# Ring slots at multiples of 256 bytes, and the result in two PSUM banks: a decode block with attention and a gated MLP

## The chip, the cores and the metric

The kernel runs on one core of a Trainium2 chip. The metric is the device time of one execution in microseconds (us); a run's time is compared as the median of several. The engines are named as in the profile: PE (matmul), PEld (its weight loads), DVE, ACT and POOL (vector, scalar and general engines) and SP, whose queue issues nearly all loads.

## The reference, cut to what matters

One token with 576 features is normalized. The sum of three things is the output: the token itself, attention over the last 4096 entries of a cache, and a gated MLP.

```python
xn = layernorm(x)                                   # x: 1 x 576
q = (xn @ wq)                                       # 32 heads of 128
k, v = k_cache[:, :, -4096:], v_cache[:, :, -4096:] # 16 heads, each for two of q
o = softmax(q k^T * 128 ** -0.5) v
A = o.reshape(1, 4096) @ wo                         # wo: 4096 x 576
z = gelu(xn @ w_in)                                 # 4608
g = w_sp * layernorm(z[2304:]) + b_sp
B = (z[:2304] * g) @ w_out                          # w_out: 2304 x 576
out = x + A + B                                     # 1 x 576, bf16
```

All is bf16. One execution must read 51 MB: wq 4.7, K 16.8, w_in 5.3, V 16.8, w_out 2.7 and wo 4.7.

## The kernel before, in words

**Loads.** All large loads are issued by SP, in the order in which they are written in the code (lines 76 to 106): wq in two pieces; K for four heads; w_in in three pieces; then K and V in turn, two heads (2,048 KB) to a load; w_out in one piece; wo in six pieces of 9, 8, 6, 4, 3 and 2 rows for each partition. Each load goes to a slot of a ring (`ring_tile`, L70) of RING = 7 slots, each of 20,736 bytes in every partition. A load waits until the readers of its slot's last contents are done. In the tile pools' order (const, work, ring, ktpool) the ring begins after the constants and the work tiles, and its first slot lies at byte 45,440 of each partition, which is 128 past a multiple of 256. A row of wo is 1,152 bytes, 4.5 times 256; partition p holds rows 32p to 32p + 31, so a piece that begins at an odd row begins 128 past a multiple in DRAM. The four pieces from rows 9, 17, 23 and 27 do.

**Order.** The schedule is written by hand. `for j in range(HKV)` takes the 16 K heads in turn. `t_head` (L245) transposes K on DVE in two halves; `s_head` (L253) computes scores with eight matmuls of 512 columns. Each four heads are a group: `sm_a` finds the maxima (DVE) and the exponentials (ACT), `sm_b` transposes them (DVE) and spreads them with sixteen ACT copies (`PT`, L295), `pv` (L303) multiplies them with V in 32 matmuls, and `yb` (L313 to L324) scales the result and turns it into Y. Between the first heads stand the MLP's matmuls (`z_mms`), its activation (`z_rest`) and its second normalization (`z_norm`), whose small matmul (L361) writes a corner of the accumulator's bank.

**The end.** The accumulator `acc` is one PSUM bank. The output's first 288 columns are summed in its partition 0 and the last 288 in partition 32. `out_mms` (L406) issues for each row of w_out or wo two matmuls of one weight column and 288 columns: one in the column tile at 0, one in the column tile at 32. After the last group's `pv` come two thirds of w_out (`out_hv(0)`, `out_hv(1)`, 24 matmuls), the last `yb`, the last third (12 matmuls) and the 32 rows of wo (64 matmuls). Then DVE (L429) copies the first 144 columns of the 33 partitions 0 to 32 into `res`, ACT (L430) the other 144, and two DMAs of 576 bytes, one issued by SP (L432) and one by ACT (L433), store partitions 0 and 32.

Of the kernel before, what the change touches and what calls it, by code (L numbers as in the profile page):

```python
# [8 lines left out]
FP32 = mybir.dt.float32  # L9
BF16 = mybir.dt.bfloat16  # L10
# [4 lines left out]
D = 576  # L15
# [14 lines left out]
CW = D // 2  # L30
# [3 lines left out]
RING = 7  # L34
# [5 lines left out]
def kernel(  # L40
# [14 lines left out]
    nc = tc.nc  # L55
    P = nc.NUM_PARTITIONS

    const = ctx.enter_context(tc.tile_pool(name="const", bufs=1))
    work = ctx.enter_context(tc.tile_pool(name="work", bufs=2))
    ring = ctx.enter_context(tc.tile_pool(name="ring", bufs=RING))  # L60
    ktpool = ctx.enter_context(tc.tile_pool(name="ktpool", bufs=3))
    ps_s = ctx.enter_context(tc.tile_pool(name="ps_s", bufs=1, space=bass.MemoryType.PSUM))
    ps_o = ctx.enter_context(tc.tile_pool(name="ps_o", bufs=1, space=bass.MemoryType.PSUM))
    ps_m = ctx.enter_context(tc.tile_pool(name="ps_m", bufs=1, space=bass.MemoryType.PSUM))
    ps_a = ctx.enter_context(tc.tile_pool(name="ps_a", bufs=1, space=bass.MemoryType.PSUM))

    ctx.enter_context(tc.manual_schedule())

# [19 lines left out]
    def load_n(src, per, lo, n, name):  # L88
        v = ring_tile(f"{name}{lo}", n, D)
        nc.sync.dma_start(v, src.rearrange("(p t) n -> p t n", t=per)[:, lo:lo + n, :])  # L90
        return [(lo + t, v[:, t, :]) for t in range(n)]
# [10 lines left out]
        V.update(load_kv(A_v_cache, m, "v"))  # L102
    wout_sb = load_n(B_w_out, NF, 0, NF, "wout")
    wo_sb = []
    for n in (9, 8, 6, 4, 3, 2):
        wo_sb += load_n(A_wo, 32, len(wo_sb), n, "wo")


# [2 lines left out]
    xrow = const.tile([1, D], BF16, name="xrow")  # L111
# [14 lines left out]
    ones_b = const.tile([1, P], BF16, name="ones_b")  # L126
# [28 lines left out]
    for n in range(2):  # L155
# [3 lines left out]
    ops = ps_o.tile([P, 512], FP32, name="ops")  # L159
    nc.vector.memset(ops[:], 0.0)  # L160

    mx = const.tile([P, 32], FP32, name="mx")
    nc.gpsimd.memset(mx[:], 0.0)
    lx = const.tile([P, 32], FP32, name="lx")
    nc.gpsimd.memset(lx[:], 1.0)
# [13 lines left out]
        out=junk[:], in0=x_col[:], in1=x_col[:], scale=1.0, scalar=0.0,  # L179
# [23 lines left out]
    for s, wv in wq_sb:  # L203
        for g in range(4):
            nc.tensor.matmul(  # L205
                qps[32 * g:32 * g + 2, :], lhsT=XT[:, s, :], rhs=wv[:, 512 * g:512 * (g + 1)],
                start=(s == 0), stop=(s == NS - 1), tile_position=(0, 32 * g),
# [12 lines left out]
    for k in range(4):  # L220
        for be in range(4):
            nc.tensor.matmul(
                qps2[:, k, be, :].rearrange("p (r g) -> p r g", r=2),
                lhsT=q_rep[0:NR, 2 * k + be // 2, be % 2].rearrange("p a d -> p (a d)"),
                rhs=idq, start=True, stop=True)
# [14 lines left out]
    def t_head(j):  # L240
        kT = ktpool.tile([P, NT, 2, 32, 2], BF16, name=f"kT{j}", tag="kT")
        src = K[j].rearrange("p t d -> p (t d)").bitcast(FP32)
        dst = kT[:].rearrange("p t b k e -> p (t b k e)").bitcast(FP32)
        for hf in range(2):
            nc.vector.transpose(dst[:, 1024 * hf:1024 * (hf + 1)], src[:, 1024 * hf:1024 * (hf + 1)])  # L245
        KT[j] = kT

    def s_head(j):
        g, i = divmod(j, GK)
        kv = KT.pop(j)[:].rearrange("p t b k e -> p b e t k")  # L250
        for hf in range(2):
            for be in range(4):
                nc.tensor.matmul(  # L253
                    S[g % 2][32 * i:32 * i + 8, hf, :],
                    lhsT=Qb[:, j, be].rearrange("p a h -> p (a h)"),
                    rhs=kv[:, be // 2, be % 2, 16 * hf:16 * hf + 16, :],
                    start=(be == 0), stop=(be == 3), tile_position=(0, 32 * i),
                )
# [13 lines left out]
    def sm_a(g):  # L272
        s = S[g % 2]
        nc.vector.tensor_reduce(out=mx[:, 0:1], in_=s[:], op=ALU.max, axis=mybir.AxisListType.XY)  # L274
        bk = spread(mx, mb, g, ALU.max, "m")
        nm = work.tile([P, 1], FP32, name=f"nm{g}", tag="nm")
        nc.vector.tensor_scalar_mul(nm[:], bk[:, 0:1], -SCALE)  # L277
        p = work.tile([P, 1024], BF16, name=f"p{g}", tag="p")
        nc.scalar.activation(p[:], s[:].rearrange("p a n -> p (a n)"), ACT.Exp, bias=nm[:, 0:1], scale=SCALE,  # L279
                             accum_out=lx[:, 0:1])  # L280
        st[g] = {"p": p}

    def sm_b(g):
        d = st[g]
        pt = work.tile([P, NT, 32], BF16, name=f"pt{g}", tag="pt")
        nc.vector.transpose(pt[:].rearrange("p t x -> p (t x)"), d["p"][:])  # L286
        lbk = spread(lx, lb, g, ALU.add, "l")
        rs = work.tile([P, 1], FP32, name=f"rs{g}", tag="rs")
        nc.vector.reciprocal(rs[:], lbk[:, 0:1])
        PT = work.tile([P, GK, NT, 2], BF16, name=f"PT{g}", tag="PT")  # L290
        pt4 = pt[:].rearrange("p t x -> p (t x)").bitcast(FP32).rearrange("p (t x) -> p t x", x=16)
        PT4 = PT[:].rearrange("p i t h -> p (i t h)").bitcast(FP32).rearrange("p (i t) -> p i t", i=GK)
        for i in range(GK):
            for a in range(4):
                nc.scalar.copy(PT4[32 * a:32 * a + 32, i, :], pt4[32 * i:32 * i + 32, :, a])  # L295
        d["PT"] = PT
        d["rs"] = rs
# [29 lines left out]
    def z_mms():  # L327
        zps = ps_a.tile([P, 2, NF], FP32, name="zps", tag="a")
        for s, wv in win_sb:
            wt = wv.rearrange("k (p t) -> k t p", t=NF)  # L330
            for t in range(NF):
                nc.tensor.matmul(zps[:, :, t], lhsT=wt[:, t, :], rhs=XT[:, s, :],  # L332
                                 start=(s == 0 and t == 0), stop=(s == NS - 1 and t == NF - 1),
                                 skip_group_check=True)
        return zps
# [21 lines left out]
        )  # L357
        return G, sz

    def z_norm(G, sz, psz):  # L360
        nc.tensor.matmul(psz[:, 0:2], lhsT=ones_f[:], rhs=sz[:], start=True, stop=True)  # L361
        mz = const.tile([P, 4], FP32, name="mz")
        nc.vector.tensor_scalar_mul(mz[:, 0:2], psz[:, 0:2], 1.0 / FH)
        nc.vector.tensor_mul(mz[:, 2:3], mz[:, 0:1], mz[:, 0:1])
        nc.vector.tensor_sub(mz[:, 2:3], mz[:, 1:2], mz[:, 2:3])
        nc.vector.tensor_scalar_add(mz[:, 2:3], mz[:, 2:3], EPS)
        nc.gpsimd.tensor_tensor(out=mz[:, 3:4], in0=mz[:, 2:3], in1=mhalf[:], op=ALU.pow)
        zn = const.tile([P, NF], FP32, name="zn")
        nc.vector.tensor_scalar(out=zn[:], in0=G[:, 1], scalar1=mz[:, 0:1], scalar2=mz[:, 3:4],
                                op0=ALU.subtract, op1=ALU.mult)  # L370
        nc.vector.tensor_scalar(out=zn[:], in0=zn[:], scalar1=wb[:, 0:1], scalar2=wb[:, 1:2],
                                op0=ALU.mult, op1=ALU.add)
        hv = const.tile([P, NF], BF16, name="hv")
        nc.vector.tensor_mul(hv[:], G[:, 0], zn[:])
        return hv

    for j in range(HKV):
        t_head(j)
        g, o = divmod(j, GK)
        if g > 0 and o == 0:  # L380
            sm_a(g - 1)
        if g > 0 and o == 1:
            sm_b(g - 1)
        s_head(j)
        if j == GK - 1:
            zps = z_mms()
        if j == GK + 1:
            G, sz = z_rest(zps)
            acc = ps_a.tile([P, 512], FP32, name="acc", tag="a")
            out_t = acc[:, 0:CW]  # L390
            nc.vector.memset(out_t, 0.0)
        if j == GK + 2:
            hv = z_norm(G, sz, acc[:, 384:386])
            for n in range(2):
                nc.tensor.matmul(
                    out_t[32 * n:32 * n + 1, :], lhsT=ones_b[:, 0:1], rhs=xrow[:, CW * n:CW * (n + 1)],
                    start=True, stop=False, tile_position=(0, 32 * n),
                )
        if g > 1 and o == 0:
            yb(g - 2)  # L400
        if g > 0 and o == 3:
            pv(g - 1)

    def out_mms(lhs, col, wv, last):
        for n in range(2):
            nc.tensor.matmul(  # L406
                out_t[32 * n:32 * n + 1, :], lhsT=lhs[:, col:col + 1], rhs=wv[:, CW * n:CW * (n + 1)],
                start=False, stop=last, tile_position=(0, 32 * n),
            )

    def out_hv(c):
        for t, wv in wout_sb[6 * c:6 * c + 6]:
            out_mms(hv, t, wv, False)
# [10 lines left out]
    for t, wv in wo_sb:  # L424
        out_mms(Y, t, wv, t == 31)

    res = const.tile([P, CW], BF16, name="res")
    half = CW // 2
    nc.vector.tensor_copy(res[0:33, 0:half], out_t[0:33, 0:half])  # L429
    nc.scalar.copy(res[0:33, half:CW], out_t[0:33, half:CW])  # L430
    out_row = out.flatten_outer_dims()
    nc.sync.dma_start(out_row[:, 0:CW], res[0:1, :])  # L432
    nc.scalar.dma_start(out_row[:, CW:D], res[32:33, :])  # L433

# [1 line left out]
_INS = ['A_x', 'A_k_cache', 'A_v_cache', 'A_wq', 'A_wo', 'B_x', 'B_w_in', 'B_w_sp', 'B_b_sp', 'B_w_out']  # L436
# [26 lines left out]
```

## Time and profile before

| What | Value |
|---|---|
| Time, median of 3 runs | 129.92 us (129.87 to 129.98) |
| Time of the profiled execution | 130.34 us |
| Its span, first to last instruction | 128.6 us |
| Mean granted clock of PE | 0.795 of full |
| PE, DVE, ACT busy | 74.6, 74.2, 23.2 us |
| Loaded | 50.96 MB |
| Mean rate over the span | 396 GB/s |
| Last wo piece (2 rows), issue to landing | 11.8 us |
| Stores issued at | 126.37 us |

The profiled execution's own time is longer than its span by the 1.74 us around the first and the last instruction, and longer than the median by 0.42 us. Times inside the profile count from the first instruction. An engine's busy time says little by itself: what matters is which wait ends last in each stage.

Two kinds of record are used beside the views. Each DMA packet has a queue, a start, a size and a duration. Each matmul has a start; its end is modelled, so the distance between starts says how fast matmuls follow one another.

### The profile page before, as it was taken

The numbers are of one execution on the slowest core, as the hardware profiler recorded it, in microseconds if no ns is written. First come the engines' busy times: TensorE is split into PE (matmuls) and PEld (weight loads), VectorE is DVE, ScalarE is ACT, GpSimd is POOL, SyncE is SP. The second block draws the span as 40 slices with busy tenths as digits, with TensorE's granted clock in tenths as the row PEclk, the third lists the DMA queues.
The fourth block names the chain that finished last, engine by engine and source line by source line (L and its number), as shares of the span: only waits on it lengthen the run. The fifth ranks groups of instructions, "written<-read, shape, count | busy, mean of one in ns | idle before, by whom it ended". The sixth has DMA issues, their size and how long they took to land.

```text
span 128.6 us, 1586 instructions
## 1 busy us (share of the span) xinstructions
PE 74.6 (58%) x610; PEld 33.4 (26%) x610; DVE 74.2 (58%) x156; ACT 23.2 (18%) x77; POOL 3.6 (3%) x19
## 2 busy tenths in 40 slices
PE   0002831399999696008459456991579802876681
PEld 0002301132699521002113111231113301234340
DVE  6604135999000599464399799997998557050000
ACT  1200011000000003920000308303074049100000
POOL 4301000000000000000100000000000000000000
PEclk9999997569995559955867976999555995589677
DMA  5999999999999999999999999999999999999940
GB/s 115 421 434 423 410 426 421 443 426 426 430 403 426 410 418 426 415 423 428 421 421 423 423 423 418 418 426 415 421 426 415 423 444 437 412 417 411 409 159 0
DMA packets 6177, 51.06 MB, mean 397 GB/s; under 512 B 535, under 2 KB 538, under 8 KB 1050
## 3 DMA queue, kind: packets, MB, share of 16 engines
q1 hardware_dynamic: 6082, 50.96, 95.3%
q8 instruction: 5, 0.08, 0.3%
q10 hardware_dynamic: 88, 0.00, 0.0%
q14 instruction: 2, 0.02, 0.0%
HBM read 50.96 MB, written 0.00 MB: 396 GB/s over the span
## 4 chain that ended last, share of the span: by engine, by line
issue 41%; DMA 28%; DVE 15%; PE 8%; ACT 4%; POOLq 0%; POOL 0%; SPq 0%; ACTq 0%; DVEq 0%
DMA k<-in_A_k_cache_dram 12%; DMA wo<-in_A_wo_dram 9%; DMA x<-in_A_x_dram 7%; DVE kT L245 6%; PE S L253 4%; ACT PT L295 3%; PE ops L303 2%; DVE pt L286 2%; DVE mx L274 2%; ACT p L279 1%; DVE on L317 1%; DVE om L313 1%; PE yps L320 1%; PE ps_x L182 0%; POOLq L458 0%
## 5 line engine op out<-in xcount | busy, mean ns | idle before, releaser
L253 PE MATMUL S<-kT,Qb 128*8 128x512 bf16 x128 | 40.8, 491 | 21.5 <-DVE kT L245 20.8
L245 DVE STREAM_TRANSPOSE kT<-k 128x1024 f32<-128x1024 f32 x32 | 37.1, 1212 | 11.1 <-DMA k<-in_A_k_cache_dram 11.0
L253 PEld LDWEIGHTS <-Qb 128*8 128x8 bf16 x128 | 11.7, 98 | 46.6 <-issue 38.2
L295 ACT COPY PT<-pt 32x32 f32<-32x32 f32 x64 | 15.4, 241 | 13.7 <-DVE pt L286 12.9
L279 ACT ACTIVATE p<-S,nm 128x1024 bf16<-128x1024 f32 x4 | 4.5, 1114 | 55.6 <-DVE nm L277 55.6
L303 PE MATMUL ops<-v,PT 128*8 128x512 bf16 x128 | 13.4, 456 | 0.4 <-ACT PT L295 0.4
L332 PEld LDWEIGHTS <-win 128*128 128x128 bf16 x162 | 10.1, 162 | 0.4 <-issue 0.4
L332 PE MATMUL zps<-XT,win 128*128 128x2 bf16 x162 | 10.2, 202 | 0.0
L320 PE MATMUL yps<-on,sel 128*32 128x32 f32 x32 | 2.1, 220 | 10.2 <-DVE on L317 10.2
L406 PE MATMUL acc<-wo,Y 128*1 128x288 bf16 x64 | 6.3, 348 | 2.8 <-DMA wo<-in_A_wo_dram 2.7
L274 DVE TENSOR_REDUCE mx<-S 128x1 f32<-128x1024 f32 x4 | 4.8, 1206 | 1.7 <-PE S L253 1.6
L429 DVE CAST res<-acc 33x144 bf16<-33x144 f32 x1 | 0.3, 299 | 9.5 <-PE acc L406 9.5
L172 PE MATMUL ps_x<-x,rmat 64*128 64x9 bf16 x1 | 0.2, 163 | 9.7 <-DMA x<-in_A_x_dram 9.7
L286 DVE STREAM_TRANSPOSE pt<-p 128x1024 bf16<-128x1024 bf16 x4 | 4.8, 1210 | 1.4 <-ACT p L279 1.4
L303 PEld LDWEIGHTS <-PT 128*8 128x8 bf16 x128 | 4.1, 91 | 5.9 <-issue 2.2
L313 DVE SCALAR_TENSOR_TENSOR om<-ops,rs,dmask 128x512 f32<-128x512 f32 x4 | 3.0, 742 | 4.2 <-PE ops L303 4.2
L406 PEld LDWEIGHTS <-Y 128*1 128x1 bf16 x64 | 3.3, 97 | 5.7 <-issue 3.9
L320 PEld LDWEIGHTS yps<-on,sel 128*32 128x32 f32 x32 | 1.7, 132 | 11.7 <-DVE on L317 9.6
L205 PE MATMUL qps<-wq,XT 128*2 128x512 bf16 x36 | 4.0, 627 | 1.0 <-DVE XT L196 1.0
L317 DVE TENSOR_REDUCE on<-om 128x128 f32<-128x512 f32 x4 | 4.1, 1030 | 0.1
L216 DVE CAST q_rep<-qps 128x512 bf16<-128x512 f32 x2 | 1.4, 692 | 4.6 <-PE qps L205 3.9
L214 ACT CAST q_rep<-qps 128x512 bf16<-128x512 f32 x2 | 1.2, 585 | 14.8 <-DVE q_rep L216 14.8
(90 smaller groups left out, 37.1 us busy)
## 6 DMA issues: line engine op xcount, KB each, us to landing
k<-in_A_k_cache_dram SPq DMA_DIRECT2D x8, 2048.0 KB, 22.3
v<-in_A_v_cache_dram SPq DMA_DIRECT2D x8, 2048.0 KB, 21.5
win<-in_B_w_in_dram SPq DMA_DIRECT2D x3, 1728.0 KB
wout<-in_B_w_out_dram SPq DMA_DIRECT2D x1, 2592.0 KB
wq<-in_A_wq_dram SPq DMA_DIRECT2D x1, 2560.0 KB
wq<-in_A_wq_dram SPq DMA_DIRECT2D x1, 2048.0 KB, 13.3
wo<-in_A_wo_dram SPq DMA_DIRECT2D x1, 1296.0 KB
wo<-in_A_wo_dram SPq DMA_DIRECT2D x1, 1152.0 KB
```

What stands on the lines that cost most here:

```text
L245: nc.vector.transpose(dst[:, 1024 * hf:1024 * (hf + 1)], src[:, 1024 * hf:1024 * (hf + 1)])
L253: nc.tensor.matmul(S[g % 2][32 * i:32 * i + 8, hf, :], lhsT=Qb[:, j, be].rearrange("p a h -> p (a h)"), rhs=kv[:, be // 2, be % 2, 16 * hf ...
L274: nc.vector.tensor_reduce(out=mx[:, 0:1], in_=s[:], op=ALU.max, axis=mybir.AxisListType.XY)
L279: nc.scalar.activation(p[:], s[:].rearrange("p a n -> p (a n)"), ACT.Exp, bias=nm[:, 0:1], scale=SCALE, accum_out=lx[:, 0:1])
L286: nc.vector.transpose(pt[:].rearrange("p t x -> p (t x)"), d["p"][:])
L295: nc.scalar.copy(PT4[32 * a:32 * a + 32, i, :], pt4[32 * i:32 * i + 32, :, a])
L303: nc.tensor.matmul(ops[32 * i:32 * i + 8, :], lhsT=d["PT"][:, i, 4 * tb:4 * tb + 4, :].rearrange("p t h -> p (t h)"), rhs=V[GK * g + i][:, ...
L313: nc.vector.scalar_tensor_tensor(out=om[:].rearrange("p c d -> p (c d)"), in0=ops[:], scalar=d["rs"][:, 0:1], in1=dmask[:].rearrange("p c ...
L317: nc.vector.reduce_sum(on[:], om[:].rearrange("p c d -> p d c"), axis=AXX)
L320: nc.tensor.matmul(yps[32 * g:32 * g + 32, :], lhsT=sel[:, dq, :], rhs=on[:, 32 * dq:32 * dq + 32], start=(dq == 0), stop=(dq == 3), tile_ ...
L332: nc.tensor.matmul(zps[:, :, t], lhsT=wt[:, t, :], rhs=XT[:, s, :], start=(s == 0 and t == 0), stop=(s == NS - 1 and t == NF - 1), skip_gr ...
L406: nc.tensor.matmul(out_t[32 * n:32 * n + 1, :], lhsT=lhs[:, col:col + 1], rhs=wv[:, CW * n:CW * (n + 1)], start=False, stop=last, tile_pos ...
```

## The change

The ring's pool is opened first, behind a pool of one tile (`mx`, 128 bytes), so that the first slot lies at byte 16,640, a multiple of 256; as a slot is 81 times 256 bytes, every slot does. The pieces of wo have 10, 8, 6, 4, 2 and 2 rows, so that each begins at an even row. The accumulator is two tiles of one partition in two PSUM banks; both use the column tile at 0. There is no fill with zeros: the two matmuls with x open the sums, and they stand before the scores of head 6 rather than after them and the norm's matmul. The norm's matmul has a bank of its own. DVE copies the first half and ACT the second, 288 columns each, into one row, which SP stores with one DMA of 1,152 bytes.

```diff
+    lead = ctx.enter_context(tc.tile_pool(name="lead", bufs=1))
+    ring = ctx.enter_context(tc.tile_pool(name="ring", bufs=RING))
     const = ctx.enter_context(tc.tile_pool(name="const", bufs=1))
     work = ctx.enter_context(tc.tile_pool(name="work", bufs=2))
-    ring = ctx.enter_context(tc.tile_pool(name="ring", bufs=RING))
...
+    ps_b = ctx.enter_context(tc.tile_pool(name="ps_b", bufs=1, space=bass.MemoryType.PSUM))
...
-    for n in (9, 8, 6, 4, 3, 2):
+    for n in (10, 8, 6, 4, 2, 2):
         wo_sb += load_n(A_wo, 32, len(wo_sb), n, "wo")
...
-    mx = const.tile([P, 32], FP32, name="mx")
+    mx = lead.tile([P, 32], FP32, name="mx")
...
-    def z_norm(G, sz, psz):
+    def z_norm(G, sz):
+        psz = ps_m.tile([P, 512], FP32, name="psz", tag="m")
...
-            acc = ps_a.tile([P, 512], FP32, name="acc", tag="a")
-            out_t = acc[:, 0:CW]
-            nc.vector.memset(out_t, 0.0)
+            acc = [ps_a.tile([1, 512], FP32, name="acc0", tag="a"), ps_b.tile([1, 512], FP32, name="acc1")]
+            for n in range(2):
+                nc.tensor.matmul(acc[n][:, 0:CW], lhsT=ones_b[:, 0:1], rhs=xrow[:, CW * n:CW * (n + 1)],
+                                 start=True, stop=False)
         if j == GK + 2:
-            hv = z_norm(G, sz, acc[:, 384:386])
-            for n in range(2):
-                nc.tensor.matmul(
-                    out_t[32 * n:32 * n + 1, :], lhsT=ones_b[:, 0:1], rhs=xrow[:, CW * n:CW * (n + 1)],
-                    start=True, stop=False, tile_position=(0, 32 * n),
-                )
+            hv = z_norm(G, sz)
...
         for n in range(2):
-            nc.tensor.matmul(
-                out_t[32 * n:32 * n + 1, :], lhsT=lhs[:, col:col + 1], rhs=wv[:, CW * n:CW * (n + 1)],
-                start=False, stop=last, tile_position=(0, 32 * n),
-            )
+            nc.tensor.matmul(acc[n][:, 0:CW], lhsT=lhs[:, col:col + 1], rhs=wv[:, CW * n:CW * (n + 1)],
+                             start=False, stop=last)
...
-    res = const.tile([P, CW], BF16, name="res")
-    half = CW // 2
-    nc.vector.tensor_copy(res[0:33, 0:half], out_t[0:33, 0:half])
-    nc.scalar.copy(res[0:33, half:CW], out_t[0:33, half:CW])
-    out_row = out.flatten_outer_dims()
-    nc.sync.dma_start(out_row[:, 0:CW], res[0:1, :])
-    nc.scalar.dma_start(out_row[:, CW:D], res[32:33, :])
+    res = const.tile([1, D], BF16, name="res")
+    nc.vector.tensor_copy(res[:, 0:CW], acc[0][:, 0:CW])
+    nc.scalar.copy(res[:, CW:D], acc[1][:, 0:CW])
+    nc.sync.dma_start(out.flatten_outer_dims(), res[:])
```

## The prediction

> **What bounds the kernel now.** I read first the slices of the page (busy shares, granted clock, DMA), then the DMA queues, then the last steps of the chain that ended last, then the timeline of the last 15 us.
>
> The slices: PEclk is the granted TensorE clock in tenths, DMA the mean busy share of the 16 DMA engines.
>
> ```profile
> PEclk9999997569995559955867976999555995589677
> DMA  5999999999999999999999999999999999999940
> GB/s 115 421 434 423 410 426 421 443 426 426 430 403 426 410 418 426 415 423 428 421 421 423 423 423 418 418 426 415 421 426 415 423 444 437 412 417 411 409 159 0
> ...
> q1 hardware_dynamic: 6082, 50.96, 95.3%
> ```
>
> The reader is to see that the DMA engines are busy from the second slice to the 38th, at 403 to 444 GB/s: SP's queue never runs dry. The time is the stream of 51 MB, plus a head, plus what follows its last byte.
>
> The chain in order of time (start, duration, what):
>
> ```profile
> 66.92 16.02 DMA k<-in_A_k_cache_dram
> ...
> 113.49 11.76 DMA wo<-in_A_wo_dram
> 125.25 0.04 issue
> 125.29 0.43 PE acc L406 x4
> 125.72 0.02 issue
> 125.74 0.31 DVE res L429
> 126.05 0.02 issue
> 126.07 0.27 ACT res L430
> ```
>
> The last wo piece lands at 125.25 though it was issued at 113.49: 11.8 us of queue stand before it, so compute that frees a slot a little later costs nothing. ACT's copy starts when DVE's has ended. Earlier, DVE waits for K at 66.92 to 82.94, and from there the chain to the last PV matmul (113.05) is compute.
>
> The timeline of PE in the same stretch (start, duration, group, count, idle before and its releaser):
>
> ```profile
> 114.26 1.39 PE L406 MATMUL acc<-wout,hv 128*1 128x288 bf16 x19 [0.83 <-DMA wout<-in_B_w_out_dram]
> ...
> 117.20 1.27 PE L406 MATMUL acc<-wo,Y 128*1 128x288 bf16 x18 [0.57 <-DMA wo<-in_A_wo_dram]
> ...
> 119.99 4.20 PE L406 MATMUL acc<-wo,Y 128*1 128x288 bf16 x36 [1.52 <-DMA wo<-in_A_wo_dram]
> ...
> 125.29 0.41 PE L406 MATMUL acc<-wo,Y 128*1 128x288 bf16 x4 [0.18 <-DMA wo<-in_A_wo_dram]
> ```
>
> PE waits for DMA before each piece: the 100 output matmuls now fit between landings. They do so because two run at once: in the records the two halves of a row start 3 to 5 ns apart, and the next pair 122 ns later (114.264, 114.267, then 114.386, 114.389).
>
> **The change, part by part.**
>
> *Ring slots.* The first slot moves from byte 45,440 (128 past a multiple of 256) to 16,640 (a multiple); slots are 20,736 bytes, itself a multiple, so all seven move alike. The packet records give bytes and duration. Their commonest durations are 309 ns for 8,192 bytes, 516 to 521 for 13,824, 761 for 20,480, 93 for 2,304. Slope: (761 - 309) / 12,288 = 0.0368 ns a byte; what is left at zero bytes is 309 - 301.3 = 7.7 ns a packet. All these are written 128 past a multiple. The two result packets (576 bytes, from 64 past) took 27 ns, leaving 5.8; the x row (1,152 bytes, to 160 past) 51 ns, leaving 8.6. So 64, 128 and 160 bytes leave 5.8, 7.7 and 8.6 ns: a line with 0.03 ns a byte, which at zero leaves 3.9. A start on the multiple would then save 3.8 ns, or 128 x 0.0368 = 4.7 if each skipped byte costs its transfer time. A DMA engine moves 352 data packets (16 wq, 256 K and V, 24 win, 8 wout, 48 wo): 1.3 to 1.7 us. Bounds: nothing, if the remainder belongs to the direction (the 64-byte case is a store) and not to the start; all 7.7 ns, 2.7 us. I take 4.6 ns, the nearest rows: 1.6 us at the end, 1.4 at wout (304 packets), 1.0 at the K load that ends at 82.94 (216 packets).
>
> The Trainium skill's DMA: Bandwidth & Descriptors, in How a descriptor splits into AXI transactions, has a read that starts off a 256-byte multiple pay for the bytes before its start, four beats of 32 bytes here, 4.7 ns at its 850 MHz; it speaks of reads, and a load writes the ring. The same page, under Where 436 GB/s comes from, holds that loads from HBM are bound at about 358 GB/s by HBM, by which the alignment of the SBUF side would be worth nothing. This trace's 421 to 426 GB/s in most slices is above that bound, so I do not follow it.
>
> *wo pieces.* Rows 9, 17, 23 and 27 are 128 past a multiple in DRAM, and those pieces become even. Their packets (347, 262, 178, 135 ns for 9,216 to 3,456 bytes) lie within 1 ns of the line of the pieces from aligned rows, so the source alone is worth 0, at most 32 packets x 4.7 = 0.15 us, inside the above. The last piece stays two rows.
>
> *Two banks.* Both halves now write partition 0, in one column tile, so a pair runs one after the other. The score matmuls (L253), one after another in one column tile, start 217 ns apart for 512 columns at full clock (28.219, 28.436, 28.652): 0.424 ns a column, 122 ns for 288, and 427 at half clock. Their step from one bank to the other (28.868 to 29.055) adds nothing. 100 matmuls take 99 x 0.122 + the last one's 0.285 = 12.36 us. Before, that was 11.43 (114.26 to 125.70), waits included. **PE becomes the bound of the end**: the landing of wout starts it, no later landing matters. Bound from below: 6.1 us if they still overlapped, when DMA would set the end again.
>
> *Clock.* The granted clock falls after idle stretches and rises after busy ones:
>
> ```profile
> 113.28:116.69 3.41, 2.52 (x45) 1.65 (x44) 2.00 (x3) 0.00 (x0) 0.00 (x0) 1.00 0.99 420
> 116.69:120.11 3.42, 1.39 (x21) 0.88 (x21) 0.00 (x0) 0.00 (x0) 0.00 (x0) 1.00 1.00 414
> 120.11:123.52 3.41, 3.29 (x28) 1.68 (x25) 0.00 (x0) 0.00 (x0) 0.00 (x0) 0.50 0.89 355
> ```
>
> (Columns: stretch, length, busy time of PE, PEld, DVE, ACT and POOL, granted clock, DMA share, GB/s.) PE worked 1.39 us in the second stretch, and the third had half clock. With PE busy without a break from PV on, that fall should go. But PV itself starts at half clock after 6 us without much work, and where the steps of 3.41 us lie relative to it is chance. 0 to 2 us of the output stage can run at half speed, at half of that lost: 0 to 1.0, I take 0.2.
>
> *Preparation.* DVE's fill of the accumulator (0.298 us at 56.9) goes; DVE later idles 11 us for K, so 0. The two x matmuls come earlier on PE and wait for DVE's copy out of zps; behind them stand the scores of head 6, which need transposes that DVE does later still. The norm's small matmul gets a bank of its own. 0; uncovered, some 0.3.
>
> *Copies.* Before: end of PE at 125.70 to store at 126.37 = 0.67. Now DVE and ACT copy 288 columns side by side. DVE: 299 ns for 144, 692 for 512 columns, so 453; ACT: 272 and 585, so 395. DVE starts one matmul (0.12) earlier; ACT ends last, 0.03 + 0.395: 0.42 in all, a gain of 0.25. If they still went one after the other: 0.9, a loss of 0.2.
>
> *Store.* One issue by SP with 1,152 bytes for two with 576; SP's own was the later to land (127.62). 0, within 0.1 either way.
>
> **Sum.** wout lands at 114.22 - 1.4 = 112.82; PV would end at 113.05 - 1.0 = 112.05, so wout starts PE at 112.86. PE ends at 112.86 + 12.36 = 125.22, 0.48 before the old 125.70. Clock +0.2, the Y matmuls now in line +0.05, copies -0.25: -0.5. The profiled execution took 130.34 us (span 128.6 and 1.74 around it), so 129.8; the runs' median 129.92 is 0.42 below it, so **129.4**.
>
> **Rivals.**
>
> *Alignment buys nothing (slower).* The remainder of 7.7 ns belongs to loads as such; for it, only loads show it, and the packets of 2, 4 and 18 bytes all take 9 ns wherever they start. Then wout lands at 114.22, PE ends at 114.26 + 12.36 = 126.62, 0.92 late; clock +0.1, Y 0.05, copies -0.25: +0.8, **130.7**. It decides where wout gains under 0.8 us, 2.7 ns a packet. Chance 0.25.
>
> *The clock is late.* The gain is there, but PV straddles two steps and 2 us of the output stage go at half clock: 1.0 for 0.2, +0.3, **130.2**. For it, PV at 109.87 to 113.05 ran wholly at half clock; against, only the worst phase costs that. Chance 0.1.
>
> *The whole remainder goes.* 7.7 ns a packet: wout lands 2.3 earlier, PV ends 1.7 earlier, PE begins at 111.96: **128.5**. Chance 0.1.
>
> *Mine*: 0.55, from 129.0 to 130.0.
>
> **How the numbers follow.** 0.2% (0.26 us) is about what a measurement can tell from no change. Of mine, three quarters lie below 129.66 and nearly all the rest within; the last rival is faster, the first two slower: faster 0.51, same 0.14, slower 0.35. Range 128.7 to 131.0: it takes in the slower cases and most of the fastest.
>
> **What would show it.** Commonest packet of 8,192 bytes at 304 to 305 ns, wout landing near 112.8; output matmuls 122 ns apart with no wait for wo; DVE and ACT copies side by side; no half clock after PV. I am wrong if 309 stays, if PE waits for wo again, or if pairs still start together.

## The result, and the profile after

The changed kernel takes 129.45 us (median of 22 runs, 129.13 to 130.32); the kernel before, beside it, 130.05 us (22 runs). The ratio is 0.9961, with an interval of 0.9948 to 0.9974: 0.4% faster. A later set of 12 runs on another occasion gave 0.9945 (0.9927 to 0.9962).

The profiled execution took 129.18 us with a span of 127.4. The slices of its page, and its DMA queue:

```profile
PEclk9999995558975555555955999679769995599999
DMA  4999999999999999999999999999999999999920
GB/s 135 437 416 427 412 427 432 443 434 421 434 408 432 422 419 430 427 430 427 427 430 427 430 427 430 422 424 430 427 427 430 424 461 452 396 408 429 407 107 0
...
q1 hardware_dynamic: 6082, 50.96, 94.9%
```

The DMA engines are still always busy, but the long middle stretch stands mostly at 427 to 430 GB/s where it stood mostly at 415 to 426. The chain that ended last no longer ends on a wo piece (start, duration, what):

```profile
112.44 0.04 issue
112.49 2.67 PE acc L407 x21
115.16 0.10 PE yps L323 x3
115.25 0.03 PE acc L407
115.28 0.06 PE yps L323 x2
115.35 9.56 PE acc L407 x78
124.91 0.02 issue
124.93 0.39 ACT res L428
```

wout lands at 112.44 instead of 114.22, and from there 100 matmuls run without a pause to 124.9. The last wo piece lands at 123.49 (before: 125.25), 1.4 us before PE has finished: nobody waits for it. The timeline of the same stretch (start, duration, group, count, idle before and releaser):

```profile
112.49 2.73 PE L407 MATMUL acc<-wout,hv 128*1 128x288 bf16 x21 [0.58 <-DMA wout<-in_B_w_out_dram]
...
116.89 8.00 PE L407 MATMUL acc<-wo,Y 128*1 128x288 bf16 x64
124.81 0.45 DVE L427 CAST res<-acc 1x288 bf16<-1x288 f32 x1 [8.92 <-PE acc L407]
124.93 0.39 ACT L428 CAST res<-acc 1x288 bf16<-1x288 f32 x1 [16.34 <-PE acc L407]
125.35 0.31 SPq L429 DMA_DIRECT2D out_dram<-res  x1
```

The 64 wo matmuls have no idle time before them and start 122 to 123 ns apart in the records, one by one. The two copies overlap, each waiting for PE alone.

The packet records hold the surprise. Packets of 8,192 bytes (the loads of K and V) take 309 ns, as their shortest did before; but now 4,088 of 4,096 do, where 1,322 did, and the mean falls from 314.0 to 309.4. The shortest time, which the prediction had fall to 304 or 305, has not moved.

### The profile page after: what moved, and what is told of

Its sections match the earlier page's. It is cut to its first block, busy times and chain, and to the rows that moved or that the text cites. A ratio compares the mean times of both kernels' runs of the same rounds, so it can differ in the third digit from the quotient of the medians.

```text
span 127.4 us, 1582 instructions
## 1 busy us (share of the span) xinstructions
PE 79.6 (62%) x610; PEld 37.2 (29%) x610; DVE 74.0 (58%) x155; ACT 23.3 (18%) x77; POOL 3.6 (3%) x19
## 4 chain that ended last, share of the span: by engine, by line
issue 40%; DMA 27%; PE 21%; DVE 9%; POOLq 0%; POOL 0%; ACT 0%; SPq 0%
DMA wout<-in_B_w_out_dram 20%; PE acc L407 10%; PE S L256 7%; DMA x<-in_A_x_dram 7%; DVE kT L248 4%; PE ops L306 3%; DVE pt L289 1%; DVE on L320 1%; DVE om L316 1%; PE ps_x L185 0%; POOLq L455 0%; PE yps L323 0%; POOL mv L191 0%; ACT res L428 0%; DVE zn L375 0%
## 5 line engine op out<-in xcount | busy, mean ns | idle before, releaser
L256 PE MATMUL S<-kT,Qb 128*8 128x512 bf16 x128 | 42.0, 507 | 20.9 <-DVE kT L248 20.3
L306 PE MATMUL ops<-v,PT 128*8 128x512 bf16 x128 | 15.0, 497 | 0.4 <-ACT PT L298 0.4
L407 PE MATMUL acc<-wo,Y 128*1 128x288 bf16 x64 | 8.0, 286 | 0.0
L407 PEld LDWEIGHTS <-Y 128*1 128x1 bf16 x64 | 5.4, 84 | 2.5
L407 PE MATMUL acc<-wout,hv 128*1 128x288 bf16 x36 | 4.6, 286 | 0.6 <-DMA wout<-in_B_w_out_dram 0.6
L208 PE MATMUL qps<-wq,XT 128*2 128x512 bf16 x36 | 3.5, 561 | 0.7 <-DVE XT L199 0.7
L407 PEld LDWEIGHTS <-hv 128*1 128x1 bf16 x36 | 3.1, 85 | 2.4 <-issue 1.2
```

The source lines that it names most:

```text
L208: nc.tensor.matmul(qps[32 * g:32 * g + 2, :], lhsT=XT[:, s, :], rhs=wv[:, 512 * g:512 * (g + 1)], start=(s == 0), stop=(s == NS - 1), tile ...
L256: nc.tensor.matmul(S[g % 2][32 * i:32 * i + 8, hf, :], lhsT=Qb[:, j, be].rearrange("p a h -> p (a h)"), rhs=kv[:, be // 2, be % 2, 16 * hf ...
L306: nc.tensor.matmul(ops[32 * i:32 * i + 8, :], lhsT=d["PT"][:, i, 4 * tb:4 * tb + 4, :].rearrange("p t h -> p (t h)"), rhs=V[GK * g + i][:, ...
L407: nc.tensor.matmul(acc[n][:, 0:CW], lhsT=lhs[:, col:col + 1], rhs=wv[:, CW * n:CW * (n + 1)], start=False, stop=last)
```

## The experiments

The prediction had said what would show it wrong, and one of those signs was there: 309 stayed. So two theories stood against each other for the faster stream. S: the slot's start decides whether all packets take their shortest time. P: the ring's new place in the memory, or the pools' order, does it. And theory B said that the serial matmuls gave back part of the gain.

**e1: the kernel before, with aligned slots alone.**

```diff
+    lead = ctx.enter_context(tc.tile_pool(name="lead", bufs=1))
     ring = ctx.enter_context(tc.tile_pool(name="ring", bufs=RING))
...
+    pad = lead.tile([P, 32], FP32, name="pad")
+    nc.gpsimd.memset(pad[:], 0.0)
```

> The kernel before with one tile of 128 bytes ahead of the ring, and nothing else: the slots begin at multiples of 256 bytes, 128 bytes further up; the wo pieces still begin at odd rows, and the end of the kernel is the old one. Theory S (the start of the slot decides whether packets of one size all take their shortest time): packets of 8,192 bytes all near 309 ns instead of a mean of 314, wout lands near 112.5 us, the last wo piece near 123.5; as the old end hangs on that landing, the time falls by 1.6 to 1.8 us, to 128.3. Theory P (it was the new place of the ring in the memory, 28,800 bytes further down, or the order of the pools): packets as before, 130.0. If the odd rows in DRAM matter by themselves, only the packets of 9,216, 6,912, 4,608 and 3,456 bytes keep their spread.

Measured: 128.48 us, ratio 0.988 (0.9867 to 0.9892). 4,087 of 4,096 packets of 8,192 bytes took 309 ns; wout landed at 112.17, the last wo piece at 123.25. The wo packets from odd rows took their shortest time too (9,216 bytes: 347 ns in 127 of 128; 6,912 and 4,608 bytes: all). So S holds: 128 bytes of padding, with the rest of the code left, are worth 1.6 us, and the start in DRAM is worth nothing. The padding also moves the pool behind the ring (the transposed K) by 128 bytes. That is not the cause: this pool begins at a multiple of 256 in e1 (byte 190,720) and in e5 below (191,232), and e5's packets are slow. The timeline of its end shows PE waiting for DMA again before two of the pieces, and the two old copies one after the other:

```profile
118.13 1.15 PE L409 MATMUL acc<-wo,Y 128*1 128x288 bf16 x16 [1.13 <-DMA wo<-in_A_wo_dram]
...
120.19 3.62 PE L409 MATMUL acc<-wo,Y 128*1 128x288 bf16 x30 [0.92 <-DMA wo<-in_A_wo_dram]
...
123.86 0.30 DVE L432 CAST res<-acc 33x144 bf16<-33x144 f32 x1 [8.34 <-PE acc L409]
124.19 0.27 ACT L433 CAST res<-acc 33x144 bf16<-33x144 f32 x1 [14.89 <-DVE res L432]
```

This smallest edit is already 1 us faster than the whole change.

**e2: the change without the alignment.**

```diff
-    mx = lead.tile([P, 32], FP32, name="mx")
+    mx = lead.tile([P, 64], FP32, name="mx")[:, 0:32]
```

> The changed kernel with the lead tile 256 bytes long instead of 128, so that all slots begin 128 past a multiple of 256; the rest of the change stays. Theory S: packets of 8,192 bytes spread from 309 to 321 ns again, wout lands near 114.2, the serial output matmuls end 0.9 late, time 130.7. Theory P: the place is the new one, so packets stay at 309 and the time at 129.45.

Measured: 130.80 us, ratio 1.0065 (1.0046 to 1.0083): slower than before. The packets of 8,192 bytes spread again (309 in 1,415 of 4,096, mean 313.9), though the ring lies within 128 bytes of its new place. P falls. The timeline is that of the prediction's first rival:

```profile
114.01 2.73 PE L407 MATMUL acc<-wout,hv 128*1 128x288 bf16 x21 [1.43 <-DMA wout<-in_B_w_out_dram]
...
118.41 8.00 PE L407 MATMUL acc<-wo,Y 128*1 128x288 bf16 x64
126.33 0.45 DVE L427 CAST res<-acc 1x288 bf16<-1x288 f32 x1 [8.92 <-PE acc L407]
```

PE starts late with wout, has the same 12.4 us of serial work, and ends at 126.4.

**e3: the change with two column tiles.**

```diff
-            acc = [ps_a.tile([1, 512], FP32, name="acc0", tag="a"), ps_b.tile([1, 512], FP32, name="acc1")]
+            acc = [ps_a.tile([1, 512], FP32, name="acc0", tag="a")[:, 0:CW],
+                   ps_b.tile([33, 512], FP32, name="acc1")[32:33, 0:CW]]
...
-            nc.tensor.matmul(acc[n][:, 0:CW], lhsT=lhs[:, col:col + 1], rhs=wv[:, CW * n:CW * (n + 1)],
-                             start=False, stop=last)
+            nc.tensor.matmul(acc[n], lhsT=lhs[:, col:col + 1], rhs=wv[:, CW * n:CW * (n + 1)],
+                             start=False, stop=last, tile_position=(0, 32 * n))
...
```

> The changed kernel with the second half of the sums in partition 32 of its own bank, in the column tile at 32, so that the two matmuls of a row can run at once; DVE and ACT still copy side by side into one row. Theory B (the serial matmuls bound the end of the changed kernel): pairs start 3 to 5 ns apart, PE waits for the wo pieces again and the last one ends 0.4 after the last landing (123.49), near 123.9 instead of 124.9: 1.0 us less, 128.5. Rival (PE is no bound there, or moving a row from partition 32 to 0 costs what is won): 129.4.

Measured: 128.42 us, ratio 0.9874 (0.986 to 0.9888). The timeline:

```profile
115.87 1.39 PE L408 MATMUL acc<-wo,Y 128*1 128x288 bf16 x20 [0.89 <-DMA wo<-in_A_wo_dram]
...
118.59 1.14 PE L408 MATMUL acc<-wo,Y 128*1 128x288 bf16 x16 [1.33 <-DMA wo<-in_A_wo_dram]
...
123.44 0.41 PE L408 MATMUL acc<-wo,Y 128*1 128x288 bf16 x4 [0.27 <-DMA wo<-in_A_wo_dram]
...
123.88 0.45 DVE L428 CAST res<-acc 1x288 bf16<-1x288 f32 x1 [9.33 <-PE acc L408]
123.92 0.39 ACT L429 CAST res<-acc 1x288 bf16<-1x288 f32 x1 [15.45 <-PE acc L408]
```

20 matmuls take 1.39 us instead of some 2.6, PE waits for every piece, and the copies start 0.9 us earlier. B holds. ACT moves partition 32 to partition 0 in the same 0.39 us. This version beats both kernels, as e1 does; run again as e11 it gave the same.

> The kernel of e3 as it is, for more runs beside the other two: median near 128.4, span 126.5; around the span 2 of its 4 runs so far were above 1.95, and by both theories some of these are too.

Measured: 128.39 us, ratio 0.9878 (0.9865 to 0.9891); e1 and e3 can't be told apart by their medians (128.48 and 128.42). The median spans, from first to last instruction, are 126.7 and 126.5 us, so the new copies and the single store are worth some 0.2 us at most where DMA sets the end; part of that can be the clock, which in e1's profile is 0.57 of full from 120 to 124 us.

**e5 and e6: how the price goes with the distance.** e3 with the lead tile at 192 and at 160 bytes (`[P, 48]` and `[P, 40]`, of which `mx` is the first 32 columns).

> The kernel of e3 (aligned slots, two column tiles, end set by DMA: 128.42 us) with the lead tile 192 bytes long, so that all slots begin 64 past a multiple of 256. Theory S1 (any start off a multiple of 256 brings the spread, as at 128 past): packets of 8,192 bytes at a mean of 314, time 128.42 + 1.7 = 130.1. Theory S2 (the price grows with the distance, as skipped bytes would): half of it, a mean near 311.5 and 129.2. Theory S3 (only 128 past is bad): 128.4.

> As e5, with the lead tile 160 bytes long: slots begin 32 past a multiple of 256. S1: 314 and 130.1. S2: a quarter, a mean near 310.5 and 128.8. S3: 128.4.

Measured, packets of 8,192 bytes and time:

| Slots begin past a multiple of 256 by | Kernel | 309 ns in, of 4,096 | Commonest | Mean, ns | Time, us |
|---|---|---|---|---|---|
| 0 | e3 | 4,089 | 309 | 309.6 | 128.42 |
| 32 | e6 | 345 | 313 | 314.9 | 130.30 |
| 64 | e5 | 410 | 312 | 314.2 | 130.03 |
| 128 | before | 1,322 | 309 | 314.0 | 130.02 |

(The kernel of the last row has the old end, which by e1 and e3 costs 0.1 us in the time and 0.2 in the span.) The price does not grow with the distance: S2 falls, and so does S3. Any of the three starts costs 1.6 to 1.9 us, the nearest one most. Why most packets then take 2 to 12 ns more, and the others not, the records don't say. The rule of the Trainium skill that the prediction named (DMA: Bandwidth & Descriptors, How a descriptor splits into AXI transactions), stretched from reads to writes, would have each packet pay for the bytes before its start: an estimate from the page's 32-byte beats at 850 MHz is 1.2, 2.4 and 4.7 ns for 32, 64 and 128 bytes. The runs show 5.3, 4.6 and 4.4 in the mean and nothing in the shortest, so the measurement decides against that form of it.

For the other direction, a read of SBUF, there is one witness: the packet of 1,152 bytes that stores the result. The lead tile moves its row too, to 64, 96, 128 and 192 bytes past a multiple of 256 (e3, e6, e5, e2), and it took 48, 49, 51 and 53 ns. That is one packet each, and it rises by 0.04 ns a byte: here the price does grow with the distance.

**e4 and e7: the clock.** Both add matmuls of 512 columns into a free bank, so that PE does not rest before the last PV: e4 20 before the last `yb`, e7 34 there and 8 more after PV. `keep_busy(n)` issues n of them; e7's edit at that place:

```diff
+    keep_busy(34)
     yb(g - 1)
     pv(g)
+    keep_busy(8)
```

> The changed kernel with 20 more matmuls of 512 columns between the last score matmuls and the last yb, into a bank that nobody reads then: work added, so that PE does not rest before the last PV. Theory C (runs of the changed kernel from 129.1 to 130.3 us differ by how long the half clock lasts into the output stage): full clock from PV on, the slow runs near 130.1 vanish, median near 129.2. Rival (the spread has another cause): median 129.45 and the same spread; or later by up to 0.5 where the added matmuls hold PV up.

e4 measured 129.22 us, ratio 0.9936 (0.9924 to 0.9947), but did not do what it should: the added matmuls ended at 104.3, PE rested to 106.7, and the granted clock fell to a half at 107.9, just before PV. It can't decide theory C.

> The changed kernel with 34 added matmuls of 512 columns before the last yb and 8 between the last PV and wout, into a bank that nobody reads then: work added. In e4 PE rested from 104.2 to 106.7 us and PV still ran at half clock, so e4 did not do what it was to do. Theory C (the spread of the changed kernel's runs is the clock's): PV runs at full clock, in 1.8 us instead of 3.3, no half clock in the output stage in any run, all runs near 129.2, none above 129.6. Rival (another cause): some of the runs lie near 130.1 as before. If the added matmuls themselves start at half clock and hold PV up, the runs lie higher, by up to 1 us.

e7 measured 129.15 us, ratio 0.9933 (0.9918 to 0.9948). The stretches before PV, with PV, and with the output matmuls (columns as in the prediction: length, five engines, granted clock, DMA), first of e7:

```profile
104.00:108.00 4.00, 3.68 (x27) 1.58 (x25) 2.82 (x9) 3.62 (x15) 0.00 (x0) 1.00 1.06 453
108.00:112.40 4.40, 3.41 (x38) 1.38 (x39) 1.78 (x2) 0.25 (x2) 0.00 (x0) 1.00 0.98 419
112.40:125.00 12.60, 12.40 (x108) 8.38 (x107) 0.48 (x2) 0.16 (x1) 0.00 (x0) 1.00 0.77 318
```

and of the changed kernel:

```profile
104.00:108.00 4.00, 0.82 (x11) 0.52 (x11) 3.10 (x9) 3.29 (x14) 0.00 (x0) 0.58 1.04 446
108.00:112.40 4.40, 3.51 (x32) 0.94 (x30) 0.50 (x2) 0.57 (x3) 0.00 (x0) 0.61 0.99 420
112.40:125.00 12.60, 12.41 (x108) 8.39 (x107) 1.72 (x4) 0.07 (x1) 0.00 (x0) 1.00 0.75 311
```

With a full clock PV ends at 110.0 instead of 111.7, and the time does not change, since wout lands at 112.35 all the same. The output stage has the full clock in both.

> The changed kernel as it is, beside e7 on the same chip: median 129.45, runs from 129.1 to 130.3, by theory C and by its rival alike; it is there for the spread.

e8 measured 129.30 us (12 runs, 129.00 to 130.38). The spans settle theory C: each run comes with the span of its own execution, and those of the changed kernel lie between 127.2 and 127.8 us in all 34 runs, e7's between 127.2 and 127.6. The runs at 130.0 to 130.4 have the same spans as the others; what is longer is the time around the span. C falls, though e7's six runs (128.97 to 129.44 us) came out as it had said.

**e9 and e10: the time around the span.** It is 1.75 to 1.92 us in the 29 runs of the kernel before beside e5 to e8, and 1.76 to 1.85 in e1's 4. In the changed kernel it is above 1.95 in 13 of 34 runs, six of them at 2.69 to 2.88; in the 11 runs of e4 and e7 it is never above 1.92. e9 is e3 with two stores (SP and ACT), e10 is e3 with one more constant tile, which e4 and e7 also had.

> The kernel of e3 with the row stored by two DMAs again, DVE's half by SP and ACT's half by ACT, each after its own copy. In kernels with the new end some runs are longer by up to 1.1 us though their span from first to last instruction is the same: the time around the span is 1.75 to 1.92 us in all runs of the kernel before, and 1.75 to 2.88 with the new end. Theory T (the single store by SP, with no DMA of ACT at the end, lets the time around the span vary): all runs within 1.75 to 1.95 around the span; in the span 0 to 0.1 less, as SP no longer waits for ACT. Rival U (it is something else, such as the place of tiles or of code): some runs above 1.95 as in e3.

> The kernel of e3 with one more constant tile of 1,024 bytes, filled by POOL at the start and read by nobody. e4 and e7 had this tile beside their added matmuls, and none of their 11 runs was above 1.92 around the span. Theory T: no effect, some runs above 1.95. Rival U (place of tiles or of code): none above 1.95. The span stays at 126.5 either way.

e9: 128.55 us, ratio 0.989 (0.9872 to 0.9908); one of 6 runs had 2.46 us around the span, so T falls as put. Its span was no shorter (126.65 against 126.5). e10: 128.38 us, ratio 0.987 (0.9856 to 0.9885); one of 4 runs had 2.10, so U in the form of this tile falls too. The cause stays open.

## Why the prediction was right, and where it was not

**The result.** 129.4 was forecast, 129.45 measured, and the place of the gain and of the loss were the forecast ones: an earlier wout, then PE as the bound. The four kernels of two edits show it (in brackets the median span; that of the kernel before is from the 11 runs beside e1 and e2):

| Time, us | Old end | New end (serial matmuls) |
|---|---|---|
| Slots 128 past | 130.05 (128.3), before | 130.80 (128.8), e2 |
| Slots aligned | 128.48 (126.7), e1 | 129.45 (127.4), the change |

Alignment is worth 1.6 and 1.35 us, the new end costs 0.75 and 0.97. By the spans the new end costs only 0.5 and 0.7; most of the rest is the time around the span, whose median is 1.79 us in the kernel before and in e1, 1.92 in the changed kernel and 1.99 in e2, for a cause that is open. So the agreement to 0.05 us is partly luck. The span fell by 0.8 to 0.9 where the sum had 0.5, mostly because the clock's 0.2 did not come and the store took 0.13 less; and the time around the span, which the sum left as it was, grew.

**The alignment: right size, wrong mechanism.** By the prediction's own sign (309 stays) this step was wrong. It read the 7.7 ns that a packet has left at zero bytes as a price of its start, and took 4.6 ns of it as gained. The 7.7 ns stayed whole: 309, 516, 771 and 93 ns are the shortest times in both kernels. The x row, now 32 past instead of 160, took 51 ns as before (53 in e9, 51 in every other profile). So in a load the remainder does not go with the start in SBUF, as the first rival said. The stores, one of the three points of its line, are the other direction: the new one of 1,152 bytes, again from 64 past, left 5.6 ns as those of 576 bytes had left 5.8, and there the start does count (48 to 53 ns, above). A price of the kind that the step put on loads shows in the store alone. What went was another thing, which the step didn't price though the records had it: the excess of packets over their shortest time. It was 314.0 - 309.4 = 4.6 ns in the mean for the 256 K and V packets of an engine, 1.2 us, with some 0.2 from the others. That the two figures agree is chance. The stream gained 1.76 us between the two profiles; but the profiled execution of the kernel before was one with a span of 128.6, and the median span of its runs is 128.2 to 128.3. By medians, e1 against the runs beside it, the gain is 1.6 in the span. One more reading of the step was loose: 18 of the 37 full slices before stand at 421 to 426 GB/s, not most; the lowest, 403, is above the 358 GB/s that the step set aside all the same.

**The serial matmuls: right.** 122 ns apart, 12.36 us forecast, with 0.05 for the Y matmuls, and 12.42 measured (112.49 to 124.91); e3 gave back 1.0 us of time, 0.9 of span.

**The copies: right.** 0.42 us from PE's end to the store forecast, 0.44 measured (124.91 to 125.35), DVE 447 ns against 453, ACT 387 against 395. **The store**: issue to landing 1.12 us instead of 1.25, just past the 0.1 that was allowed.

**The clock: mis-sized.** 0.2 was taken for half clock in the output stage. It was 0: in both profiles of the changed kernel (the first and e8) that stage has the full clock, and the spans of 34 runs differ by 0.6 us at most, where the second rival needed a loss of 1.0. That rival is not seen. The fall that the step expected to go, the half clock at 120.11, did go.

**wo pieces: right at 0.** e1 kept the odd rows and lost nothing. **Preparation: 0 fits.** It was not tried alone; e1 has the old one and e3 the new one, and they lie 0.1 apart.

**The first rival** needed a stream that does not gain. It was made in e2: 130.7 forecast, 130.80 measured, of which some 0.2 is time around the span. **The third**, that the whole 7.7 ns goes, fell with the 309 that stayed.

## What to carry to other kernels

Where a kernel is bound by its loads, look at the packet records for how many packets of one size take their shortest time; if few do, look where their tiles begin, and pad them to a multiple of 256 bytes. Opening the ring's pool first was not enough: e2 does that too, and its slots begin 128 past. A gain in the stream is only worth what the next bound leaves: count what follows the landing, in series, before giving up matmuls that run side by side. And test each part of a change alone: here 128 bytes of padding beat the whole.

## What was not expected of the hardware

- The start of a tile in SBUF does not change the shortest time of a packet that is written there, but how many packets take longer: 0.2% at a multiple of 256, 65 to 92% at 32, 64 and 128 past (packets of 8,192 bytes). A store of 1,152 bytes took longer the further past a multiple its row began in SBUF: 48 ns at 64, 53 at 192.
- The completions of the last load's 16 DMA engines lie 1.5 to 2.1 us apart: 2.13 in the kernel before, 1.96 in the changed one, 1.54 in e1, 1.77 in e5. That is as much as alignment gained, and it does not go with it: kernels with aligned slots (1.54 to 1.96) and without (1.77 to 2.13) overlap. Its cause was not tried.
- The time outside the span varies by 1.1 us between runs of the changed kernel with equal spans, and hardly in the kernel before; its cause is open.
